# Decode attention for two models on one core: `wq` of B loaded ahead of the first block of keys, three products ahead of the first sum, and one tail transfer cut in two

## The chip, the cores and the metric

One core of a Trainium2 chip runs the whole program; the other cores are idle. The metric is the time of one execution on the device in microseconds (us). The core has five engines with queues of their own (TensorE or PE, VectorE or DVE, ScalarE or ACT, GpSimd or POOL, SyncE or SP) and a set of 16 DMA engines. They are ordered by semaphores alone: an instruction, or an engine's queue, waits until a counter has reached a value.

## The reference

Two independent attention layers, A and B, decode one token each: 32 heads of 128, a cache of 8192 keys and values per head, bf16.

```python
def attention(x, k_cache, v_cache, wq, wo):          # A and B alike
    q = (x @ wq).reshape(1, 1, 32, 128).transpose(0, 2, 1, 3)          # x: 1x1x512, wq: 512x4096
    scores = einsum("bhqd,bhkd->bhqk", q, k_cache) * 128 ** -0.5       # k_cache: 1x32x8192x128
    p = softmax(scores, axis=-1)
    o = einsum("bhqk,bhkd->bhqd", p, v_cache)
    return o.transpose(0, 2, 1, 3).reshape(1, 1, 4096) @ wo            # wo: 4096x512
out = concatenate([attention(A...), attention(B...)], axis=-1)         # 1x1x1024
```

With one query per head, every byte of the two caches is used once. The caches, `wq` and `wo` together are 285 MB.

## The kernel before, in words

The 64 heads are taken four at a time: 16 steps, called quads here (A's are 0 to 7, B's 8 to 15). A quad has 8.39 MB of keys (K0 to K15) and 8.39 MB of values (V0 to V15), each loaded with one DMA on SP's queue: 32 partitions per head, 256 cache positions per partition. `kn` holds two blocks of keys (even and odd quads), `vn` one block of values. Before the first values come, `vn` holds `wq` of A and of B (4.19 MB each), and a row at the start of the odd half of `kn` (`xrow`) holds `x` of A and B. At the end `wo` lies over `kn`.

What the engines do:

- **q.** In `pe_first`, PE spreads `x` over the partitions (line 326 before), ACT copies it to `xb` (354), and PE forms q of A and then of B with 16 matmuls for each half of the heads (336); after each half ACT copies the result to `qbc` (359, four copies), and PE's next half waits for these copies.
- **Scores of a quad.** DVE multiplies the keys with q in place in four chunks of 64 positions (`mul`, line 408). PE adds the products of one chunk with 16 matmuls against the identity (244 and 247) into one of two banks of `big`, and DVE adds up the last 8 columns into `s_sb` (`sr`, line 413). PE's chunk c waits for product c (`s_mul`) and for the `sr` that has freed its bank (`s_sr`).
- **Softmax.** DVE takes the maximum, ACT the exponentials (371).
- **Values.** After the score sums of quad n PE multiplies the probabilities of quad n-1 with its values (64 matmuls, line 294), ACT copies the result (365) and PE turns it into columns (300).
- **Output.** B's `wo` comes in six transfers (`WOB`); the last heads are multiplied in `rows` (219), after the last values.

SP's queue sets the order of the loads, and each load waits until its place is free: K(n+1) for the first product of quad n, V(n) for the value matmuls of quad n-1 (`s_pv`). At the start the order is `wq` of A, `x`, K0, `wq` of B (which waits for `wq` of A), K1 (which waits for the first product of quad 0), V0 (which waits for all of q, since `wq` lies in `vn`), K2 (which waits until all of quad 0 is summed, `s_red`, and K1 is there), V1, and so on. At the end V15 comes in two parts (`s_v` and `s_v1`, 192 and 64 positions), and PE waits for the second part after 48 of its 64 matmuls (`VCUT`).

The program text that the change touches, with the line numbers of the profile:

Of the kernel before, what the change touches and what calls it, by code (L numbers as in the profile page):

```python
# [11 lines left out]
P = 128  # L12


def bass_concat_heads__mha_block_cached__gqa_block_cached__decode_kernel(
# [18 lines left out]
    NA = 2  # L34
# [7 lines left out]
    G = 4  # L42
# [19 lines left out]
    RG = [32, 16, 8, 4, 2]  # L62
    VCUT = T - CT
# [3 lines left out]
    with ExitStack() as st:  # L67
# [53 lines left out]
        s_x, s_w, s_k, s_v, s_v1, s_out = [sem("s_" + x) for x in ("x", "w", "k", "v", "v1", "out")]  # L121
# [50 lines left out]
        def load_k(n, *needs):  # L172
            load(flat(kn[:, (n % 2) * T:(n % 2 + 1) * T, :]), quad(ks, n), s_k, *needs)
# [4 lines left out]
        def load_wq(a, *needs):  # L178
            load(flat(vn[:])[:, a * W:(a + 1) * W], wqs[a].rearrange("(p c) n -> p (c n)", p=P),
                 s_w, *needs)  # L180

        def load_wo(a, h0, n, c, *needs):
            load(wo_sb[:, a * H + h0:a * H + h0 + n, :].rearrange("p j n -> p (j n)"),
                 wos[a][h0 * Dh:(h0 + n) * Dh, :].rearrange("(p j) n -> p (j n)", p=P), c, *needs)

        load_wq(0)
        for a in range(NA):
            load(xrow[0:1, a, :], xs[a][0], s_x)
        load_k(0)
        load_wq(1, (s_w, 16))  # L190
        for n in range(NM):
            if n + 1 < NM:
                load_k(n + 1, *([(s_red, RED), (s_k, 32)] if n == 1 else [(s_mul, NCH * n + 1)]))
                load_v(n, (s_pv, n + 1) if n else (s_q, 4 * NA * 2))
# [5 lines left out]
        for (h0, n), c in list(zip(WOB, s_wo))[1:]:  # L200
            load_wo(1, h0, n, c)
# [6 lines left out]
        with nc.body("pe_main", valid_engines=[nc.tensor.engine]):  # L208
# [26 lines left out]
            with e.Fori(0, NM + 1) as n:  # L235
# [48 lines left out]
                with e.If_ne(nr, 0):  # L284
                    e.wait_ge(s_p, n1)
                    e.matmul(misc[:, 0:G], ones_f[:], rsum[:], start=True, stop=True).then_inc(s_sum, 1)  # L286
                    e.wait_ge(s_v, rv)
                    for j in range(T // NT):
                        if j * NT == VCUT:
                            with e.If_eq(nr, NM):  # L290
                                e.wait_ge(s_v1, 16)
                        q = QB * (j % NP)
                        ts = slice(j * NT, (j + 1) * NT)
                        i = e.matmul(acc[q:q + NT * G, :], pt[:, ts, :].rearrange("p t g -> p (t g)"),  # L294
                                     vn[:, ts, :].rearrange("p t d -> p (t d)"), start=(j < NP),
                                     stop=(j >= T // NT - NP), skip_group_check=True)
                    i.then_inc(s_pv, 1)
                    e.wait_ge(s_acc, n1)
                    for t in range(NT):
                        i = e.matmul(tps[:, 0:G], acc_sb[:, t * Dh:(t + 1) * Dh],  # L300
                                     tsel[:, t * G:(t + 1) * G], start=(t == 0), stop=(t == NT - 1))
                    i.then_inc(s_turn, 1)
                e.reg_add(n1, n1, 1)
                e.reg_add(rv, rv, 16)
            e.wait_ge(s_wo[1], 16)
# [3 lines left out]
            e.wait_ge(s_wo[2], 16)  # L309
            rows(2)  # L310
            e.wait_ge(t_dve, 11)
            for g in range(3, len(WOB)):
                e.wait_ge(s_wo[g], 16)
# [3 lines left out]
        with nc.body("pe_first", valid_engines=[nc.tensor.engine]):  # L317
            for r, v in ((rw, 16), (rq, G)):
                e.reg_mov(r, v)
            e.sem_inc(s_sum, 1)  # L320
            e.sem_inc(s_turn, 1)
            e.wait_ge(s_x, 16 * NA)
# [67 lines left out]
        e.sem_inc(s_sr, 2)  # L390
        e.memset(acc, 0.0).then_inc(s_pv, 1)
# [8 lines left out]
        e.wait_ge(s_qc, 2 * G)  # L400
        with e.Fori(0, NM):
# [112 lines left out]
```

## Time and profile before

| | us |
|---|---|
| three runs, median (lowest, highest) | 683.68 (683.41 to 686.24) |
| the profiled execution | 683.11 |
| its span in the trace | 681.9 |
| PE busy | 405.0 (59%) |
| DVE busy | 338.9 (50%) |
| ACT busy | 80.9 (12%) |
| DMA queue of the loads: 285.22 MB | 97.1% of 16 engines' span |

The profiled execution is 0.57 us below the median of the runs, and 1.2 us of it lies outside the span. Times in the rows count from the span's start. In a timeline's row stand the start, the duration, the engine, the line, the operation, what it writes and reads, and how many were merged; in brackets stands how long the engine was idle before and what ended that. "SPq" is SP's queue as it issues a DMA. In a row of stretches stand the stretch, its length, each engine's busy time with its count of instructions, then the granted clock of PE (1.00 is full speed), the share of the DMA engines and their GB/s.

### The profile page before, as it was taken

What the parts mean: (1) busy time and instruction counts of PE and PEld (TensorE: products, weight loads), DVE (VectorE), ACT (ScalarE), POOL (GpSimd) and SP (SyncE); (2) the same over time, 40 slices, a digit from 0 to 9 for tenths busy, and PEclk for the clock granted to TensorE, in tenths of its full rate; (3) what the DMA queues carried; (4) which work ended last, traced back from release to release, by engine and by line L of the source; (5) the groups of instructions that cost most, each with busy time, mean ns of one, the idle gap of its engine ahead of it and who ended that gap; (6) DMA issues with size and microseconds to landing.
All of it is one profiled execution on the core that took longest, in us unless ns stands there. A gap on an engine that the chain in (4) does not pass through costs nothing.

```text
span 681.9 us, 8031 instructions
## 1 busy us (share of the span) xinstructions
PE 405.0 (59%) x2407; PEld 169.9 (25%) x2407; DVE 338.9 (50%) x218; ACT 80.9 (12%) x182; POOL 2.4 (0%) x13
## 2 busy tenths in 40 slices
PE   1526757755838284674728285573818375583886
PEld 0112223222313132231313132231313122231333
DVE  1040784916556280836547281835647291655600
ACT  1211011020020202010020202011020202002020
POOL 1000000000000000000000000000000000000000
PEclk9866879886859697796959678796958788685887
DMA  9999793999999999999999999999999999999997
GB/s 382 429 467 427 327 423 115 434 442 431 431 431 431 431 431 431 431 431 431 431 431 431 431 438 450 438 442 434 442 431 431 431 431 431 431 431 431 423 442 304
DMA packets 6064, 285.24 MB, mean 418 GB/s; under 512 B 683, under 2 KB 942, under 8 KB 1198
## 3 DMA queue, kind: packets, MB, share of 16 engines
q1 hardware_dynamic: 6056, 285.22, 97.1%
q8 instruction: 1, 0.02, 0.0%
q14 instruction: 1, 0.01, 0.0%
q10 hardware_dynamic: 6, 0.00, 0.0%
HBM read 285.21 MB, written 0.00 MB: 418 GB/s over the span
## 4 chain that ended last, share of the span: by engine, by line
DMA 74%; DVE 13%; PE 9%; issue 2%; ACT 1%; DVEq 0%; ACTq 0%; SPq 0%
DMA kn<-in_B_k_cache_dram 40%; DMA kn<-in_A_k_cache_dram 25%; DVE kn L408 12%; PE big L247 5%; DMA vn<-in_B_wq_dram 4%; DMA vn<-in_B_v_cache_dram 3%; DMA vn<-in_A_wq_dram 2%; PE big L336 2%; PE acc L294 1%; PE big L244 1%; ACT qbc L359 1%; PE tps L300 0%; PE yrow L219 0%; DVE s_sb L413 0%; DVEq L403 0%
## 5 line engine op out<-in xcount | busy, mean ns | idle before, releaser
L408 DVE TENSOR_TENSOR kn<-kn,qbc x64 | 281.5, 4419 | 123.5 <-DMA kn<-in_A_k_cache_dram 65.6
L247 PE MATMUL big<-kn,ident 128*128 x960 | 272.4, 431 | 0.0
L244 PE MATMUL big<-kn,ident 128*128 x64 | 28.5, 445 | 216.7 <-DVE kn L408 212.2
L247 PEld LDWEIGHTS big<-kn,ident 128*128 128x128 bf16 x960 | 103.6, 108 | 153.6 <-issue 101.0
L413 DVE TENSOR_REDUCE s_sb<-big 128x64 f32<-128x512 f32 x64 | 44.1, 689 | 115.4 <-PE big L247 115.4
L365 ACT COPY acc_sb<-acc 128x512 f32<-128x512 f32 x16 | 9.4, 586 | 478.8 <-PE acc L294 478.8
L244 PEld LDWEIGHTS big<-kn,ident 128*128 128x128 bf16 x64 | 6.3, 99 | 234.0 <-issue 231.8
L294 PE MATMUL acc<-vn,pt 128*16 128x512 bf16 x1024 | 58.5, 380 | 2.7 <-DMA vn<-in_B_v_cache_dram 2.7
L371 ACT ACTIVATE pt<-s_sb,negb 32x256 bf16<-32x256 f32 x64 | 54.8, 857 | 1.3
L433 DVE TENSOR_TENSOR oD<-tps,rinv 128x4 f32 x16 | 2.6, 162 | 75.8 <-PE tps L300 75.6
L336 PE MATMUL big<-vn,acc_sb 128*128 x64 | 21.1, 497 | 22.8 <-DMA vn<-in_B_wq_dram 13.4
L294 PEld LDWEIGHTS acc<-vn,pt 128*16 128x16 bf16 x1024 | 24.0, 89 | 29.2 <-issue 2.9
L300 PE MATMUL tps<-tsel,acc_sb 128*128 128x4 f32 x128 | 17.7, 262 | 11.0 <-ACT acc_sb L365 10.4
L300 PEld LDWEIGHTS tps<-tsel,acc_sb 128*128 128x128 f32 x128 | 16.3, 199 | 19.3 <-ACT acc_sb L365 17.9
L336 PEld LDWEIGHTS big<-vn,acc_sb 128*128 x64 | 7.6, 119 | 36.2 <-issue 33.5
L371 ACT ACTIVATION_READ_ACCUMULATOR pt<-s_sb,negb 32x1 f32 x64 | 15.9, 248 | 0.0
L359 ACT CAST qbc<-big 32x512 f32 x16 | 9.2, 577 | 36.6 <-PE big L336 36.3
L269 PE MATMUL big<-kn,o 128*1 x48 | 12.4, 421 | 0.0
L286 PE MATMUL misc<-rsum,ones_f 128*128 128x4 f32 x32 | 6.0, 259 | 6.9 <-issue 6.2
L367 ACT ACTIVATE negb<-gm 128x1 f32<-128x1 f32 x16 | 3.2, 203 | 48.3 <-DVE gm L436 48.3
L326 PE MATMUL misc<-ones_bf,kn 1*128 1x128 bf16 x4 | 0.6, 302 | 13.1 <-DMA kn<-in_B_x_dram 13.1
L286 PEld LDWEIGHTS misc<-rsum,ones_f 128*128 128x128 f32 x32 | 4.8, 188 | 13.8 <-issue 13.8
(48 smaller groups left out, 38.5 us busy)
## 6 DMA issues: line engine op xcount, KB each, us to landing
vn<-in_B_v_cache_dram SPq DMA_DIRECT2D x1, 6144.0 KB, 18.4
vn<-in_A_wq_dram SPq DMA_DIRECT2D x1, 4096.0 KB, 13.2
vn<-in_B_wq_dram SPq DMA_DIRECT2D x1, 4096.0 KB, 29.1
kn<-in_A_wo_dram SPq DMA_DIRECT2D x1, 4096.0 KB, 24.3
kn<-in_B_wo_dram SPq DMA_DIRECT2D x1, 2048.0 KB, 28.9
vn<-in_B_v_cache_dram SPq DMA_DIRECT2D x1, 2048.0 KB, 23.0
kn<-in_B_wo_dram SPq DMA_DIRECT2D x1, 1024.0 KB, 25.0
kn<-in_B_wo_dram SPq DMA_DIRECT2D x1, 512.0 KB, 25.8
```

Source lines behind the costliest of these rows:

```text
L244: e.matmul(o, ident[:], chunk(0), start=True, stop=False, skip_group_check=True)
L247: i = e.matmul(o, ident[:], chunk((1 + u) * DW), start=False, stop=(u == RU - 1), skip_group_check=True)
L269: i = e.matmul(y, o2[:, bass.ds(h + u, 1)], wo_sb[:, h + u, :], start=False, stop=False, skip_group_check=True)
L286: e.matmul(misc[:, 0:G], ones_f[:], rsum[:], start=True, stop=True).then_inc(s_sum, 1)
L294: i = e.matmul(acc[q:q + NT * G, :], pt[:, ts, :].rearrange("p t g -> p (t g)"), vn[:, ts, :].rearrange("p t d -> p (t d)"), start=(j < NP ...
L300: i = e.matmul(tps[:, 0:G], acc_sb[:, t * Dh:(t + 1) * Dh], tsel[:, t * G:(t + 1) * G], start=(t == 0), stop=(t == NT - 1))
L336: i = e.matmul(big[:, bass.ds(hh, 1), :].rearrange("p o (i d) -> p (o i) d", d=Dh), xb[:, a, c, :], wq_v[:, a, c, j, :, hh, :], start=(c = ...
L359: e.copy(qbc[q, bass.ds(j * 4, 4), :].rearrange("p i d -> p (i d)"), big[q, hh, :]).then_inc(s_qc, 1)
L365: e.copy(acc_sb[:], acc).then_inc(s_acc, 1)
L371: i = e.activation(pt[q, :, h], s_sb[q, :], AF.Exp, bias=negb[q, :], scale=scale, accum_out=rsum[q, h:h + 1])
L408: e.tensor_tensor(k, k, qbc[:, bass.ds(n, 1), :].broadcast_to([P, CT, Dh]), ALU.mult).then_inc(s_mul, 1)
L413: e.tensor_reduce(s_sb[:, c * CT:(c + 1) * CT], big[:, c % 2, :].rearrange("p (t d) -> p t d", d=DW), AX.X, ALU.add).then_inc(s_sr, 1)
```

## The change

Six things change.

1. SP issues `wq` of B directly behind `x` and ahead of K0, without a wait. Each `wq` has a semaphore of its own, and so has K0 (`s_k0`). K1 waits only until PE has read `x` (`s_xm`), since `xrow` lies where K1 goes; it no longer waits for a product of quad 0.
2. PE waits for `wq` of A, and in the loop for `wq` of B, with the same loop over A and B as before; DVE waits for K0 before its loop over the quads.
3. In every quad DVE makes three products ahead of its first `sr`, and the fourth between the first and the second `sr`.
4. At the end PE issues eight matmuls of a zero column ahead of the wait for the second part of V15.
5. B's `wo` of heads 24 to 27 comes in two transfers: rows 0 to 119 of the partitions and rows 120 to 127.
6. PE waits for 32 instead of 16 on that part of `wo`.

On SP the first loads stand in this order; the names are the tile that is written and the tensor that is read, and in brackets the semaphores that the load waits for. Before:

```order
L170 DMA vn<-in_A_wq_dram 128x16384 [waits barrier_Pool_Activation_PE_DVE_SP_release]
L170 DMA kn<-in_A_x_dram 1x512
L170 DMA kn<-in_B_x_dram 1x512
L170 DMA kn<-in_A_k_cache_dram 128x32768
L170 DMA vn<-in_B_wq_dram 128x16384 [waits s_w]
L170 DMA kn<-in_A_k_cache_dram 128x32768 [waits s_mul]
L170 DMA vn<-in_A_v_cache_dram 128x32768 [waits s_q]
L170 DMA kn<-in_A_k_cache_dram 128x32768 [waits s_k,s_red]
L170 DMA vn<-in_A_v_cache_dram 128x32768 [waits s_pv]
```

And after:

```order
L173 DMA vn<-in_A_wq_dram 128x16384 [waits barrier_Pool_Activation_PE_DVE_SP_release]
L173 DMA kn<-in_A_x_dram 1x512
L173 DMA kn<-in_B_x_dram 1x512
L173 DMA vn<-in_B_wq_dram 128x16384
L173 DMA kn<-in_A_k_cache_dram 128x32768
L173 DMA kn<-in_A_k_cache_dram 128x32768 [waits s_xm]
L173 DMA vn<-in_A_v_cache_dram 128x32768 [waits s_q]
L173 DMA kn<-in_A_k_cache_dram 128x32768 [waits s_k,s_red]
L173 DMA vn<-in_A_v_cache_dram 128x32768 [waits s_pv]
```

`wq` of B has moved ahead of K0 and has lost its wait, K1 waits for `s_xm` in place of `s_mul`, and K2 and V1 wait for what they waited for.

On DVE the body of the loop over the quads is, before (`kn<-kn,qbc` is a product, `s_sb<-big` an `sr`):

```order
L408 TENSOR_TENSOR kn<-kn,qbc 128x8192
L408 ISA
L408 TENSOR_TENSOR kn<-kn,qbc 128x8192
L413 TENSOR_REDUCE s_sb<-big 128x64 [waits s_red,s_p]
L416 ISA
L408 TENSOR_TENSOR kn<-kn,qbc 128x8192
L413 TENSOR_REDUCE s_sb<-big 128x64 [waits s_red]
L416 ISA
L408 TENSOR_TENSOR kn<-kn,qbc 128x8192
L413 TENSOR_REDUCE s_sb<-big 128x64 [waits s_red]
```

And after:

```order
L427 TENSOR_TENSOR kn<-kn,qbc 128x8192
L427 ISA
L427 TENSOR_TENSOR kn<-kn,qbc 128x8192
L427 ISA
L427 TENSOR_TENSOR kn<-kn,qbc 128x8192
L432 TENSOR_REDUCE s_sb<-big 128x64 [waits s_red,s_p]
L435 ISA
L427 TENSOR_TENSOR kn<-kn,qbc 128x8192
L432 TENSOR_REDUCE s_sb<-big 128x64 [waits s_red]
L435 REGISTER_ALU
L432 TENSOR_REDUCE s_sb<-big 128x64 [waits s_red]
```

The third product has moved ahead of the first `sr`, and the fourth ahead of the second.

On PE, in the last pass of the loop (`acc<-vn,pt` are the value matmuls), this stands now around the wait for the second part of V15:

```order
L309 MATMUL acc<-vn,pt 16x512 [waits s_v]
L309 MATMUL acc<-vn,pt 16x512 x47
L302 COMPARE_AND_BRANCH
L304 MATMUL big<-kn,zero 1x512 x8
L302 UNCONDITIONAL_BRANCH [waits s_v1]
L309 MATMUL acc<-vn,pt 16x512 x16
L315 MATMUL tps<-tsel,acc_sb 128x4 [waits s_acc]
```

The row of eight matmuls is new; nothing else on PE has moved.

The diff, without the renaming of semaphores:

```diff
+    WP = {2: 120}
 ...
         def load_k(n, *needs):
-            load(flat(kn[:, (n % 2) * T:(n % 2 + 1) * T, :]), quad(ks, n), s_k, *needs)
+            load(flat(kn[:, (n % 2) * T:(n % 2 + 1) * T, :]), quad(ks, n), s_k if n else s_k0,
+                 *needs)
 ...
-        def load_wo(a, h0, n, c, *needs):
-            load(wo_sb[:, a * H + h0:a * H + h0 + n, :].rearrange("p j n -> p (j n)"),
-                 wos[a][h0 * Dh:(h0 + n) * Dh, :].rearrange("(p j) n -> p (j n)", p=P), c, *needs)
+        def load_wo(a, h0, n, c, *needs, p=slice(0, P)):
+            load(wo_sb[p, a * H + h0:a * H + h0 + n, :].rearrange("p j n -> p (j n)"),
+                 wos[a][h0 * Dh:(h0 + n) * Dh, :].rearrange("(p j) n -> p (j n)", p=P)[p], c, *needs)
 ...
+        load_wq(1)
         load_k(0)
-        load_wq(1, (s_w, 16))
-        for n in range(NM):
-            if n + 1 < NM:
-                load_k(n + 1, *([(s_red, RED), (s_k, 32)] if n == 1 else [(s_mul, NCH * n + 1)]))
-                load_v(n, (s_pv, n + 1) if n else (s_q, 4 * NA * 2))
+        load_k(1, (s_xm, 2))
+        load_v(0, (s_q, 4 * NA * 2))
+        load_k(2, (s_red, RED), (s_k, 32))
+        load_v(1, (s_pv, 2))
+        for n in range(2, NM - 1):
+            load_k(n + 1, (s_mul, NCH * n + 1))
+            load_v(n, (s_pv, n + 1))
 ...
-        for (h0, n), c in list(zip(WOB, s_wo))[1:]:
-            load_wo(1, h0, n, c)
+        for g in range(1, len(WOB)):
+            cut = WP.get(g, P)
+            for p in ([slice(0, cut)] + [slice(cut, P)] * (cut < P)):
+                load_wo(1, *WOB[g], s_wo[g], p=p)
+
+        def got_wo(e, g):
+            e.wait_ge(s_wo[g], 32 if g in WP else 16)
 ...
                             with e.If_eq(nr, NM):
+                                for _ in range(8):
+                                    e.matmul(big[0:1, 0, :], zero[:], wo_sb[:, 0, :], start=True,
+                                             stop=True)
                                 e.wait_ge(s_v1, 16)
 ...
             e.wait_ge(s_xb, NA)
+            e.wait_ge(s_w[0], 16)
             with e.Fori(0, NA) as a:
-                e.wait_ge(s_w, rw)
+                e.wait_ge(s_w[1], rw)
 ...
+        e.wait_ge(s_k0, 16)
         with e.Fori(0, NM):
             e.wait_ge(s_k, rk)
 ...
             mul(0)
             mul(1)
+            mul(2)
             e.wait_ge(s_p, n1)
             sr(0)
-            mul(2)
+            mul(3)
             sr(1)
-            mul(3)
             sr(2)
             sr(3)
```

More of the change, by code (lines that the diff above doesn't have):

```diff
@@ L119, in sem @@
             return ec(nc.semaphore(name))
-        s_x, s_w, s_k, s_v, s_v1, s_out = [sem("s_" + x) for x in ("x", "w", "k", "v", "v1", "out")]
+        s_x, s_k0, s_k, s_v, s_v1, s_out = [
+            sem("s_" + x) for x in ("x", "k0", "k", "v", "v1", "out")]
+        s_w = [sem("s_w%d" % a) for a in range(NA)]
         s_woA = sem("s_woA")
@@ L317, in bass_concat_heads__mha_block_cached__gqa_block_cached__decode_kernel @@
         with nc.body("pe_first", valid_engines=[nc.tensor.engine]):
-            for r, v in ((rw, 16), (rq, G)):
+            for r, v in ((rw, 1), (rq, G)):
                 e.reg_mov(r, v)
```

10 lines of the change are left out of this document (6 added, 4 removed).

## The prediction

> **What bounds the kernel now.** I read the page first: its span and the row of the DMA engines in 40 slices.
>
> ```profile
> span 681.9 us, 8031 instructions
> ...
> DMA  9999793999999999999999999999999999999997
> ```
>
> The DMA engines are busy from end to end but for the sixth and seventh slices and the last. So I looked at these in stretches of 2 us, and at the long middle in one.
>
> ```profile
> 80.00:82.00 2.00, 2.00 (x10) 0.86 (x9) 0.13 (x1) 0.00 (x0) 0.00 (x0) 1.00 0.00 0
> ...
> 104.00:106.00 2.00, 1.64 (x7) 0.57 (x6) 2.00 (x2) 0.00 (x0) 0.00 (x0) 1.00 0.00 0
> ...
> 112.00:114.00 2.00, 2.00 (x44) 0.92 (x40) 0.00 (x0) 0.00 (x0) 0.00 (x0) 1.00 0.00 0
> ...
> 115.00:640.00 525.00, 309.72 (x1842) 130.56 (x1843) 288.13 (x164) 59.07 (x140) 0.00 (x0) 0.79 1.00 432
> ```
>
> No byte moves at 80 to 82 and at 104 to 114; from 115 on the engines stand at 1.00 and 432 GB/s, so nothing but fewer idle microseconds of the DMA engines can help there. Which loads came late is told by SP's issues, and the stream's pace by the chain that ended last (start, duration).
>
> ```profile
> 83.20 0.33 SPq L170 DMA_DIRECT2D kn<-in_A_k_cache_dram  x1
> ...
> 114.94 0.33 SPq L170 DMA_DIRECT2D vn<-in_A_v_cache_dram  x1
> ...
> 146.44 0.33 SPq L170 DMA_DIRECT2D vn<-in_A_v_cache_dram  x1
> ```
>
> ```profile
> 14.06 29.06 DMA vn<-in_B_wq_dram
> ...
> 122.09 34.10 DMA kn<-in_A_k_cache_dram
> ...
> 586.60 33.99 DMA kn<-in_B_k_cache_dram
> ```
>
> K2 (83.20) and V1 (114.94) are issued when nothing is left in the queue. The last two rows are the landings of K3 (156.19) and K15 (620.59): twelve quads in 464.40, thus 38.70 for 16.78 MB (one block 19.35). V1 and K3 took 156.19 - 114.94 = 41.25, so an issue into an empty queue costs 41.25 - 38.70 = 2.55 beyond the bytes. The first 16.78 MB (both `wq` and K0) had landed at 14.06 + 29.06 = 43.12.
>
> **The stream without a pause.** K1 would then land at 43.12 + 19.35 = 62.47, V0 at 81.82, K2 at 101.17, V1 at 120.52, K3 at 139.87, which is 16.3 before 156.19. For that K2 has to be issued by 81.82 - 2.55 = 79.27 and V1 by 98.62.
>
> **Loads at the start.** The order of `wq` and K0 changes no bytes; I cost it at nothing. `wq` of A is first as before, K0 lands at 43.12, and K1's wait on `x` is met when PE has read it, ahead of the row at 15.93 below; behind it on SP stand V0 and K2, which want to be issued far later.
>
> ```profile
> 15.93 5.36 PE L336 MATMUL big<-vn,acc_sb 128*128 x16 [1.75 <-issue]
> ...
> 24.87 1.02 PE L336 MATMUL big<-vn,acc_sb 128*128 x4 [3.58 <-issue]
> ...
> 30.77 2.38 ACT L359 CAST qbc<-big 32x512 f32 x4 [6.96 <-PE big L336]
> ...
> 33.67 8.76 DVE L408 TENSOR_TENSOR kn<-kn,qbc  x2 [29.56 <-DMA kn<-in_A_k_cache_dram]
> ...
> 44.00 4.98 PE L336 MATMUL big<-vn,acc_sb 128*128 x16 [13.36 <-DMA vn<-in_B_wq_dram]
> ...
> 62.74 0.60 PE L244 MATMUL big<-kn,ident 128*128 x1 [4.57 <-issue]
> ```
>
> q of A is ready at 30.77 + 2.38 = 33.15, and PE then waited for `wq` of B until 44.00; K0's products lay ready meanwhile and their sums began at 62.74. In the new order `wq` of B lands one K0 earlier, near 23.8, so PE goes on at once: 1.2 after the copies (the idle 3.58 less ACT's 2.38), at 34.4. From there to the first sum it takes what it took, 62.74 - 44.00 = 18.74: **first sum at 53.1**, 9.6 earlier. K0's three products (4.4 each, half of 8.76) run from 43.4 to 56.6, so the first lies ready; PE is the later one. V0, which waits for q, can go at some 50, before its need at 62.47 - 2.55 = 59.9.
>
> **Three products ahead.** A quad as it was, quad 0's end and quad 1:
>
> ```profile
> 68.64 3.40 PE L247 MATMUL big<-kn,ident 128*128 x15
> 68.70 0.69 DVE L413 TENSOR_REDUCE s_sb<-big 128x64 f32<-128x512 f32 x1 [26.27 <-PE big L247]
> ...
> 83.21 0.69 DVE L413 TENSOR_REDUCE s_sb<-big 128x64 f32<-128x512 f32 x1 [3.08 <-PE big L247]
> ...
> 85.38 8.76 DVE L408 TENSOR_TENSOR kn<-kn,qbc  x2 [0.51 <-issue]
> ...
> 90.17 0.60 PE L244 MATMUL big<-kn,ident 128*128 x1 [7.00 <-DVE kn L408]
> ...
> 96.07 0.69 DVE L413 TENSOR_REDUCE s_sb<-big 128x64 f32<-128x512 f32 x1 [1.93 <-PE big L247]
> ...
> 106.39 0.39 PE L244 MATMUL big<-kn,ident 128*128 x1 [0.74 <-DVE kn L408]
> ...
> 110.61 0.69 DVE L413 TENSOR_REDUCE s_sb<-big 128x64 f32<-128x512 f32 x1 [3.99 <-PE big L247]
> ...
> 111.26 3.63 PE L294 MATMUL acc<-vn,pt 128*16 128x512 bf16 x64
> ```
>
> PE's first chunk takes 5.9 to 6.0 (62.74 to 68.70, 90.17 to 96.07), a following one without a wait 3.5, one that waited 4.2 (106.39 to 110.61). DVE stood idle 1.93 ahead of the first `sr`; the third product fills that, and the price is that this `sr` can come later than its sums.
>
> Quad 0 new: chunks end at 59.1, 62.6 (its `sr` came at 59.8), 66.2, and the fourth, whose product ends at 64.2 and whose bank is freed at 64.9, at 70.0. Then K2 is issued: 9 us ahead of 79.27, so the pause at 80 to 84 goes.
>
> Quad 1 new: its first product starts 2.2 after (83.21 to 85.38), at 72.2; PE starts 4.8 later, at 77.0, and ends chunks at 82.9 and 86.5. Three products end at 85.4, the first `sr` at 86.1; third chunk to 90.3; fourth product to 90.5, `sr` to 91.2, fourth chunk from 91.5 to 95.7. From 85.38 to 110.61 it was 25.2, now 23.5: 1.7 shorter. The values of quad 0 end 4.3 after (111.26 + 3.63 - 110.61): **V1 issued at 100.0**, late by 1.4 against 98.62. K3 lands at 100.0 + 41.25 = 141.25: **14.9 earlier**. All later loads move with it if none is issued late: V2 was issued at 146.44, 7.2 ahead of need (156.19 - 2.55), and the same distance stays, since everything here moves together. In the later quads the 1.7 is hidden behind the stream.
>
> **Before V15.** V15 must reach the queue before B's first part of `wo` has landed.
>
> ```profile
> kn<-in_B_wo_dram SPq DMA_DIRECT2D x1, 2048.0 KB, 28.9
> ...
> kn<-in_B_wo_dram SPq DMA_DIRECT2D x2, 128.0 KB, 25.8
> ```
>
> ```profile
> 625.69 0.43 SPq L170 DMA_DIRECT2D kn<-in_B_wo_dram  x1
> ...
> 650.63 0.80 SPq L170 DMA_DIRECT2D vn<-in_B_v_cache_dram  x2
> ...
> 651.47 2.34 SPq L170 DMA_DIRECT2D kn<-in_B_wo_dram  x5
> ```
>
> That part lands at 625.69 + 28.9 = 654.6; V15 is issued at 650.63, 1.4 ahead of need (654.6 - 2.55 = 652.0), and quad 15, shorter by 1.7 or more, only adds to this. No gain and no loss. The added issue on SP is one more of 0.43 behind 651.47, over 20 us before the data come.
>
> **The tail.**
>
> ```profile
> 115.58 1.06 PE L300 MATMUL tps<-tsel,acc_sb 128*128 128x4 f32 x8 [0.69 <-ACT acc_sb L365]
> ...
> 669.12 2.77 PE L294 MATMUL acc<-vn,pt 128*16 128x512 bf16 x48 [0.30 <-DMA vn<-in_B_v_cache_dram]
> 674.24 1.32 PE L294 MATMUL acc<-vn,pt 128*16 128x512 bf16 x16 [2.35 <-DMA vn<-in_B_v_cache_dram]
> ...
> 676.24 1.87 PE L300 MATMUL tps<-tsel,acc_sb 128*128 128x4 f32 x8 [0.68 <-ACT acc_sb L382]
> ...
> 680.22 0.29 DVE L477 CAST out_q<-yrow 128x128 bf16<-128x128 f32 x1 [0.82 <-PE yrow L219]
> ```
>
> ```profile
> 672.00:674.00 2.00, 0.00 (x0) 0.00 (x0) 0.00 (x0) 0.00 (x0) 0.00 (x0) 1.00 0.94 397
> 674.00:676.00 2.00, 1.32 (x16) 0.31 (x16) 0.00 (x0) 0.40 (x1) 0.00 (x0) 0.72 0.98 403
> ```
>
> PE idles 2.35 ahead of V15's last part, the granted clock falls to 0.72 in the next stretch, and the eight column matmuls take 1.87 against 1.06 in quad 0. The new eight matmuls cost some 0.22 each (3.40 for 15), 1.8 from 671.89 on, and end 0.5 before the wait does, so they delay nothing. With the clock held, 0.8 goes in that row and a little in the others, but the last `wo` lands at 651.47 + 2.34 - 0.43 + 25.8 = 679.2 on the old time, and `out_q`, at 680.22 now, cannot begin before some 679.4. I take **0.7**, with ends 0 (clock falls anyway) and 1.1 (`wo` lands a little earlier too). The cut transfer has the same bytes; I cost it at nothing, and its bad end is a rival below.
>
> [...]
>
> **The sum.** 14.9 + 0.7 = 15.6. The profiled execution is 683.11, so 667.5 by its own time; it lies 0.57 below the median of the runs, and from 683.68 the sum gives 668.1. I say 668.0.
>
> **Rivals.**
>
> - *V1 comes in time.* If PE is 1.4 faster over the seven chunks up to V1 (its first chunk was 5.3 to 6.0 in the rows, a waiting one 3.5 to 4.2), no pause is left: 16.3 + 0.7 = 17.0, 666.7. Speaks for it: the margin is small. Against: DVE's products, which set quad 1 from its third chunk on, have no slack.
> - *V1 comes later still.* Should PE lose its clock again within quads 0 and 1, a following chunk takes 5.9 in place of 3.5; two such push V1 to 104.8 and the time to 672.9. For it: PE idles 4.5 ahead of quad 0 (row at 62.74). Against: once begun, chunks follow without a gap.
> - *The change doesn't do what it says.* If `wq` of B came no earlier for PE, the first sum would stay at 62.74, V1 would be at 109.6 and the gain 5.3 + 0.7: 677.7. Against it: the stream delivered in the order of issue (`wq` of B took 29.06, behind K0).
> - *The cut transfer goes slower than the whole one*, the case that ends on the other side. If 120 rows are not spread over the engines but go through one, 491,520 bytes at 432 / 16 = 27 GB/s take 18.2 where the whole part took 524,288 / 432 = 1.2 us. The end then waits for `wo` 17 longer: 683.68 - 14.9 + 17 = 685.8. Two engines would take 9.1 and leave 676.7; only one engine makes it slower than before. No row shows a transfer of 120 rows. [...]
>
> **How the numbers follow.** Forecast 0.61, V1 in time 0.21, V1 later 0.12, no earlier q 0.03, one engine 0.03. The range 665.8 to 670.8: below, V1 in time with 1.1 in the tail (666.3) and half a microsecond; above, V1 2 later than forecast and nothing in the tail (668.1 + 2.0 + 0.7); it leaves out most of the last three. A change of 0.5%, 3.4 us, is about what a measurement of this kernel can tell from none: faster by more 0.95, within 0.02, slower by more 0.03.
>
> **What would show it.** Right: no stretch without bytes at 80 to 84 and at most 2 us of it near 100; first sum near 53, K2 issued near 70, V1 near 100, K15 landed near 605.7; DVE's first `sr` of a quad directly behind three products; a granted clock of 1.00 in the last 10 us. Wrong: SP's V1 well after 102, a wait of PE for `wq` of B, or PE at the end waiting for `wo` for more than 1 us.

## The result, and the profile after

The changed kernel takes 674.12 us (median of 6 runs, 672.38 to 674.61) where the kernel before takes 683.70 in the same comparison: a ratio of 0.9849, interval 0.9829 to 0.987. It is faster, as forecast, by 9.6 us; the forecast was 15.6 and 668.0. Of one kernel below (the cut at row 96) a run of 1385.97, twice the time of its others, is left out.

The page of the changed kernel, span and the row of the DMA engines, and stretches of 2 us at the two places where no byte moved before. The columns of a stretch are its length, the busy time of PE, its weight loads, DVE, ACT and POOL, the granted clock, the DMA share and GB/s:

```profile
span 673.1 us, 8068 instructions
...
DMA  9999987999999999999999999999999999999898
```

```profile
80.00:82.00 2.00, 0.00 (x0) 0.00 (x0) 2.00 (x2) 0.83 (x2) 0.00 (x0) 0.50 1.06 459
...
97.00:99.00 2.00, 2.00 (x10) 0.79 (x9) 0.00 (x0) 0.00 (x0) 0.00 (x0) 1.00 0.83 360
99.00:101.00 2.00, 1.87 (x8) 0.57 (x6) 0.10 (x1) 0.00 (x0) 0.00 (x0) 1.00 0.00 0
101.00:103.00 2.00, 1.75 (x30) 1.00 (x34) 1.10 (x3) 0.00 (x0) 0.00 (x0) 1.00 0.00 0
103.00:105.00 2.00, 2.00 (x44) 0.79 (x32) 0.00 (x0) 0.00 (x0) 0.00 (x0) 1.00 0.00 0
```

The pause at 80 is gone. The stream runs dry near 98.6, where the forecast has V1's need, and a pause of over 6 us is left where the forecast left 1.4. SP's issues of K2 and V1 (start, duration), and from the chain that ended last the landings of K3 and K15:

```profile
75.40 0.33 SPq L173 DMA_DIRECT2D kn<-in_A_k_cache_dram  x1
...
105.23 0.33 SPq L173 DMA_DIRECT2D vn<-in_A_v_cache_dram  x1
```

```profile
112.38 33.97 DMA kn<-in_A_k_cache_dram
...
576.96 33.97 DMA kn<-in_B_k_cache_dram
...
641.91 29.12 DMA kn<-in_B_wo_dram
671.07 0.33 PE yrow L231 x3
671.42 0.29 DVE out_q L496
```

V1 goes at 105.23 instead of 114.94: 9.7 earlier, not 14.9. K15 lands at 576.96 + 33.97 = 610.93, 9.7 earlier than the 620.59 before. The end adds nothing to that: from K15's landing to `out_q` it was 680.22 - 620.59 = 59.63, and is 671.42 - 610.93 = 60.49. So the time splits into three pieces, and a run is told by two numbers: **V1** (when V1 is issued) and **the tail** (from K15's landing to `out_q`). The piece between them, V1 to K15's landing, is 505.6 to 506.6 in every kernel below, and from the start of `out_q` to the end it is 2.9 to 3.0.

| kernel | V1 issued | K15 landed - V1 | tail | profiled execution | median of the runs |
|---|---|---|---|---|---|
| before | 114.94 | 505.65 | 59.63 | 683.11 | 683.70 |
| forecast | 100.0 | 505.65 | 58.9 | 667.5 | 668.0 |
| changed | 105.23 | 505.70 | 60.49 | 674.37 | 674.12 |

The miss, 6.9 by the profiled executions, is 5.2 in V1 and 1.6 in the tail. The experiments take these one after the other.

### The profile page after: what moved, and what is told of

Same layout as the page of the kernel before. It is cut to its first block, busy times and chain, and to the rows that moved or that the text cites. A ratio compares the mean times of both kernels' runs of the same rounds, so it can differ in the third digit from the quotient of the medians.

```text
span 673.1 us, 8068 instructions
## 1 busy us (share of the span) xinstructions
PE 405.5 (60%) x2415; PEld 168.2 (25%) x2415; DVE 337.0 (50%) x218; ACT 80.9 (12%) x182; POOL 2.4 (0%) x13
## 3 DMA queue, kind: packets, MB, share of 16 engines
q1 hardware_dynamic: 6063, 285.22, 98.5%
## 4 chain that ended last, share of the span: by engine, by line
DMA 72%; DVE 11%; PE 10%; issue 4%; ACT 1%; SPq 1%; DVEq 0%; ACTq 0%
DMA kn<-in_B_k_cache_dram 40%; DMA kn<-in_A_k_cache_dram 25%; DVE kn L427 10%; PE big L259 5%; DMA kn<-in_B_wo_dram 4%; PE big L353 4%; DMA kn<-in_B_x_dram 2%; ACT qbc L376 1%; PE acc L309 1%; DVE s_sb L432 1%; SPq L173 1%; PE big L256 0%; DVEq L422 0%; PE tps L315 0%; ACT acc_sb L371 0%
## 5 line engine op out<-in xcount | busy, mean ns | idle before, releaser
L259 PE MATMUL big<-kn,ident 128*128 x960 | 266.3, 419 | 0.0
L256 PE MATMUL big<-kn,ident 128*128 x64 | 28.1, 440 | 216.5 <-DVE kn L427 196.4
L259 PEld LDWEIGHTS big<-kn,ident 128*128 128x128 bf16 x960 | 100.8, 105 | 149.7 <-issue 99.4
L432 DVE TENSOR_REDUCE s_sb<-big 128x64 f32<-128x512 f32 x64 | 42.7, 686 | 73.4 <-PE big L259 73.4
L256 PEld LDWEIGHTS big<-kn,ident 128*128 128x128 bf16 x64 | 6.3, 98 | 234.8 <-issue 232.9
L309 PE MATMUL acc<-vn,pt 128*16 128x512 bf16 x1024 | 60.5, 387 | 2.4 <-DMA vn<-in_B_v_cache_dram 2.4
L353 PE MATMUL big<-vn,acc_sb 128*128 x64 | 25.2, 579 | 12.9 <-issue 12.9
L315 PE MATMUL tps<-tsel,acc_sb 128*128 128x4 f32 x128 | 16.9, 255 | 11.1 <-ACT acc_sb L382 10.4
L315 PEld LDWEIGHTS tps<-tsel,acc_sb 128*128 128x128 f32 x128 | 15.5, 191 | 19.1 <-ACT acc_sb L382 17.9
## 6 DMA issues: line engine op xcount, KB each, us to landing
kn<-in_B_wo_dram SPq DMA_DIRECT2D x1, 2048.0 KB, 28.9
```

Source lines behind the costliest of these rows:

```text
L256: e.matmul(o, ident[:], chunk(0), start=True, stop=False, skip_group_check=True)
L259: i = e.matmul(o, ident[:], chunk((1 + u) * DW), start=False, stop=(u == RU - 1), skip_group_check=True)
L315: i = e.matmul(tps[:, 0:G], acc_sb[:, t * Dh:(t + 1) * Dh], tsel[:, t * G:(t + 1) * G], start=(t == 0), stop=(t == NT - 1))
L353: i = e.matmul(big[:, bass.ds(hh, 1), :].rearrange("p o (i d) -> p (o i) d", d=Dh), xb[:, a, c, :], wq_v[:, a, c, j, :, hh, :], start=(c = ...
L432: e.tensor_reduce(s_sb[:, c * CT:(c + 1) * CT], big[:, c % 2, :].rearrange("p (t d) -> p t d", d=DW), AX.X, ALU.add).then_inc(s_sr, 1)
```

## The experiments

### The parts alone

Two kernels make one part of the change in the kernel before. The first has the order of `wq` of B and K0 with its waits; the second has three products ahead of the first `sr`:

```diff
+        load_wq(1)
         load_k(0)
-        load_wq(1, (s_w, 16))
...
+        load_k(1, (s_xm, 2))
```

```diff
             mul(1)
+            mul(2)
             e.wait_ge(s_p, n1)
             sr(0)
-            mul(2)
-            sr(1)
             mul(3)
+            sr(1)
```

> The kernel before with the order of wq and K0 alone changed (and the waits that belong to it): two products ahead, no columns, wo whole. Theory: V1 moves from 114.94 to some 107.7, the hour that the changed kernel with two products had, and the whole stream with it: 684.2 - 7.2 = 677.0. Rival: the order of the loads gives less by itself, since PE's sums of quad 0 then wait for DVE's products: V1 at 110 or later, 679.3 or more.

> The kernel before with three products ahead of the first sum and nothing else. Theory: quads 0 and 1 set K2 and V1 there too; quad 0 is shorter by some 3 (all three products lie ready before PE begins), quad 1 by 1.8, so V1 is issued near 110 and the time is 679.5. By the prediction's own price of 1.7 for each quad: 680.8. Rival: PE sets both quads while it forms q late, and the time stays at 684.

And the changed kernel with the products in the old order:

> The changed kernel with two products ahead of the first sum again. Theory: quads 0 and 1 set V1, and each is longer by 1.7 to 2.4, so V1 is issued 3.4 to 4 us later, near 109, and the time is 677.8. Rival: the wait of PE for its own chunks hides the third product, V1 stays near 105 and the time at 674.1.

| kernel | K2 issued | V1 issued | tail | median (lowest to highest, runs) | ratio to before (interval) |
|---|---|---|---|---|---|
| before, `wq` order alone | 75.81 | 107.65 | 59.62 | 677.33 (675.89 to 677.84, 4) | 0.9895 (0.9868 to 0.9921) |
| before, three products alone | 81.43 | 111.26 | 58.91 | 679.26 (678.60 to 680.35, 4) | 0.9926 (0.9899 to 0.9952) |
| changed, two products ahead | 75.81 | 107.66 | 60.40 | 678.03 (676.93 to 679.28, 4) | 0.9913 (0.9888 to 0.9938) |

From K2 to V1 it is 31.7 to 31.9 with two products ahead (31.74 before) and 29.8 with three: quad 1 is 1.9 shorter, and quad 0 gains as much alone (83.20 to 81.43). The order of the loads alone takes K2 from 83.20 to 75.81. The parts are worth 6.7 and 4.7 us in the medians (683.99 before in that comparison), and the medians of all three kernels came within 0.4 of what was expected (V1 within 1.4). The tail is already seen here to be 60.4 with the rest of the change and 58.9 to 59.6 without it.

### Why V1 came at 105: the clock in q

The theory behind this run: PE's clock is low through the q halves because PE idles some 3.5 us between them, and matmuls that fill these idles hold it. The filler writes a bank that is written again later, and reads tiles that are not used yet:

```diff
+            def busy(n):
+                for _ in range(n):
+                    e.matmul(yrow, ones_bf[:], pt[:, 0:P, :].rearrange("p t g -> p (t g)"),
+                             start=True, stop=True)
+
+            e.wait_ge(c_pool, POOL)
+            busy(36)
             e.wait_ge(s_x, 16 * NA)
...
+            busy(6)
...
+                    busy(8)      # behind each q half
```

> The changed kernel with PE kept busy through the forming of q: 36 matmuls of zeros ahead of x, 6 behind it, and 8 behind each of the four halves of q, into a bank that is overwritten later. Nothing else is changed. Theory: V1 is late by 5 us against the forecast because PE forms all four halves of q at half its clock (6.1 to 6.5 us each); at full clock a half takes 3.6, the first sum begins near 48, V1 is issued near 97, ahead of its need at 98.6, and no pause of the DMA engines is left: 667.5. Rival: a half takes 6 us for another reason (the weights, the copies), or the matmuls of zeros delay it; then V1 stays at 105 or later, and the time is 674 to 677.

PE's rows of the changed kernel, the four q halves, the first sum and the first of the fourth chunk (in brackets the idle time before, and what ended it), and stretches inside the second half of A and the second half of B:

```profile
15.95 6.08 PE L353 MATMUL big<-vn,acc_sb 128*128 x16 [1.74 <-issue]
25.60 6.37 PE L353 MATMUL big<-vn,acc_sb 128*128 x16 [3.57 <-issue]
36.06 6.26 PE L353 MATMUL big<-vn,acc_sb 128*128 x16 [4.09 <-issue]
45.86 6.48 PE L353 MATMUL big<-vn,acc_sb 128*128 x16 [3.54 <-issue]
56.91 0.60 PE L256 MATMUL big<-kn,ident 128*128 x1 [4.57 <-issue]
...
71.22 0.39 PE L256 MATMUL big<-kn,ident 128*128 x1 [0.62 <-issue]
```

```profile
26.00:28.00 2.00, 2.00 (x6) 0.67 (x5) 0.00 (x0) 0.00 (x0) 0.00 (x0) 0.50 1.21 524
...
46.00:48.00 2.00, 2.00 (x6) 0.72 (x6) 2.00 (x1) 0.00 (x0) 0.00 (x0) 0.50 1.06 459
```

The same with the idles filled (the first two rows are each the first quarter of a half, four matmuls; the second stretch lies inside the first chunk of sums):

```profile
25.07 1.02 PE L362 MATMUL big<-vn,acc_sb 128*128 x4 [1.85 <-issue]
...
34.16 1.02 PE L362 MATMUL big<-vn,acc_sb 128*128 x4 [2.37 <-issue]
...
52.20 0.39 PE L256 MATMUL big<-kn,ident 128*128 x1 [2.85 <-issue]
52.44 5.26 PE L259 MATMUL big<-kn,ident 128*128 x15
```

```profile
26.00:28.00 2.00, 1.40 (x7) 0.57 (x6) 0.00 (x0) 0.00 (x0) 0.00 (x0) 1.00 1.21 524
...
54.00:56.00 2.00, 2.00 (x6) 0.76 (x5) 2.00 (x1) 0.00 (x0) 0.00 (x0) 0.50 1.06 459
```

No half waits for its weights: between two halves PE waits for ACT's copies (2.38), and its own issue ends each idle, in both kernels (`issue`: the engine waited for nothing that the profile shows). With the idles at 1.8 to 2.4 the granted clock is 1.00 in this run where it was 0.50 (26 to 28 and 46 to 48), a half goes from 6.1 to 6.5 down to 5.0 (four times 1.02 and gaps of 0.3), and the first sum comes at 52.20, not 56.91. Behind the idle of 2.85 ahead of it the clock reads 0.50 at 54 to 56, and that chunk takes 5.5. V1 goes at 100.57, K2 at 70.71, and the median is **670.01 (669.97 to 670.45, 5 runs), ratio 0.9792 (0.9773 to 0.9811)**: 4.1 below the changed kernel. I had expected V1 at 97 and 667.5, with halves of 3.6; the gaps within a half stay at full clock, so that the direction was right and V1 gained 4.7 of the 8.2.

How long q takes also moves V1 from one execution to the next. Five kernels have the unfilled q and the same code up to V1: the four halves together take 23.0 (`wo` whole), 23.2 (cut at 112), 23.8 (no columns), 25.2 (the changed one) and 25.5 (cut at 127), and V1 is issued at 102.80, 103.15, 103.86, 105.23 and 105.56, thus 79.8 to 80.1 more than this sum in all five. Eight with filled q issue it between 100.26 and 101.10. The filling doesn't bring every half down in each of them: in this kernel and one more all four halves take 5.0, and in the six others one half (with the cut at 96, two) takes 5.3 to 5.8, behind an idle of 1.9 to 2.4. In the third half of one of these, the kernel without columns, the first four matmuls still take 1.02 and the next twelve 4.44 (3.6 in this kernel):

```profile
33.84 1.02 PE L359 MATMUL big<-vn,acc_sb 128*128 x4 [2.32 <-issue]
35.18 4.44 PE L359 MATMUL big<-vn,acc_sb 128*128 x12 [0.31 <-issue]
```

The granted clock at 36 to 38 is 0.50 there. The spread of the runs is not all from q: those of the changed kernel spread over 2.2 us and those of this one over 0.5, but those of the other filled kernels over 0.2 to 2.0, and V1 to K15's landing is 506.2 to 506.6 in three of them; why is not shown.

In the changed kernel the granted clock reads 0.50 from 24.5 to 31.1, 34.7 to 41.4, 45.0 to 51.6 and 55.2 to 61.8, which is most of three halves and of the first chunk, and 1.00 at 31.3 to 34.5, 41.5 to 44.8 and 51.8 to 55.0, where PE is busy for 0.5 to 0.8 us each time. The runs don't give one length of idle that brings it down: it reads 0.50 with idles of 3.5 to 4.1 and behind the one of 2.85, and with those of 1.9 to 2.4 all four halves took 5.0 in two kernels but not in the six others. Why one execution of the same code has a longer q than the next is not shown.

One more kernel, with `wo` whole (next part), had ten more matmuls behind the last half, ahead of PE's jump to the sums:

```diff
+            busy(10)
```

> The kernel with both edits (PE busy through q, wo whole), and ten more matmuls of zeros behind the last half of q, ahead of PE's jump to its main loop. Theory: the first chunk of quad 0 took 5.3 at a granted clock of 0.50 to 0.84 after an idle 2.85; held at full speed it takes 3.6, V1 moves from 100.6 to some 98.9, and the time is 1.7 less than with both edits alone: about 665.5. Rival: the fourth product on DVE or the jump sets quad 0, V1 stays at 100, and the time is the same within 0.5.

It gives 668.58 (667.89 to 669.90, 5 runs), ratio 0.9769 (0.9748 to 0.9789), where the kernel without these ten gives 668.91: no difference. I had expected 665.5; the rival, the same within 0.5, came. Its first chunk takes 3.6 now instead of 5.5, but K2 goes at 70.44 and V1 at 100.26, within 0.8 of the 71.15 and 101.01 without them. Its second and third chunks of quad 0 begin so:

```profile
56.73 0.39 PE L256 MATMUL big<-kn,ident 128*128 x1 [0.62 <-issue]
...
61.49 0.39 PE L256 MATMUL big<-kn,ident 128*128 x1 [0.62 <-issue]
```

The chunks begin 4.2, 4.8 and 4.8 apart, although the third product was there at 56.99 and the bank free at 57.59. So PE's own issue sets quad 0 here, and from the first sum to K2 it is 17.9 with a fast first chunk and 18.5 with a slow one.

### The tail: the cut of `wo`

The changed kernel with that part of `wo` whole:

```diff
-    WP = {2: 120}
+    WP = {}
```

> The changed kernel with one edit: wo of B's heads 24 to 27 comes whole again, 128 rows. Theory: the cut costs the end of the wo stream about 1.3 to 1.6 us, and the end waits for that stream, so the last wo lands near 669.5 in place of 671.03, out_q begins near 670, and the time is 672.8 (1.3 less than the changed kernel's 674.1). Rival: the wo stream is slower for another reason (the column matmuls, or the engines of the DMA at that hour), and the time stays at 674.1.

It takes 671.09 (670.19 to 673.26, 5 runs), ratio 0.9813 (0.9791 to 0.9836). V1 is at 102.80 in its profile, 2.4 earlier since its q halves took 2.2 less, so the median's 3.0 is not all the cut's. The tail tells the two apart: K15 lands at 608.44, `out_q` is at 667.31, 58.87 against 60.49. Its end, from the chain:

```profile
664.56 1.07 PE tps L315 x8
...
666.26 0.18 PE big L224
666.44 0.85 PE yrow L231 x27
667.31 0.29 DVE out_q L496
```

PE and DVE follow each other without a wait for `wo`; in the changed kernel the last row of PE waits for the last transfer of `wo` (the chain above).

Is it the cut at 120, or any cut? My guess, which no row shows, was that a transfer of 120 rows goes over 15 engines and one of 8 rows over 8, so that the shares of the engines become uneven; cuts at 112, 96 and 64 leave both parts a multiple of 16. And a cut at 127 asks for the case that the prediction feared.

```diff
-    WP = {2: 120}
+    WP = {2: 112}     # and, each in a kernel of its own, 127
```

> The changed kernel with the cut at 112 in place of 120: transfers of 112 and of 16 rows, as many transfers as before, both of a multiple of 16 rows. Theory 1, the cut costs because of the number of engines (15 and 8 in place of 16): with 16 for both, the wo stream is as fast as whole, the last wo 5.1 behind V15's last part, and the time is 671.1 to 671.5. Theory 2, one more transfer or an uneven share of rows costs: the last wo is 6 or more behind, and the time 673 to 674.

> The changed kernel with the cut at 127: transfers of 127 rows and of 1 row. This is the prediction's rival of one engine, made on purpose: if a transfer of 127 rows goes through one engine, 520 KB at 27 GB/s take 19.3 in place of 1.2, and the time is 674 + 17 = 691, the last wo some 23 behind V15's last part. If the number of rows does not set the number of engines, it stays at 674.

The next four share the filled q (with the ten matmuls behind it) and have no column matmuls; the first leaves `wo` whole, the others cut it.

> The kernel with PE busy through q and up to its jump, and wo whole, now without the eight columns. Theory: with V1 early PE's 48 matmuls run at a low clock and the columns only stand in the way of the last 16; without them these begin at the landing, and the end comes 1 earlier: 667.6. Rival: without them the clock is low in the eight column matmuls behind and the gain is given back: 668.6.

> The kernel without columns (PE busy through q, wo otherwise whole) with the cut at 120. The last wo then sets the end. Theory 1, 15 engines with another share of rows are slow: the last wo lands 29.2 to 29.5 after its issue in place of 27.9, and the time is 1.5 to 2 more than without the cut. Theory 2, one transfer more costs: the same here, so it is told apart by the next two.

> The same with the cut at 96: transfers of 96 and 32 rows, both of a multiple of 16. Theory 1 (the engine count of 15): 27.9 to 28.1. Theory 2 (one transfer more): 28.3 or more. [...]

> The same with the cut at 64: two transfers of 64 rows, both of a multiple of 16. Theory 1 (the engine count of 15): as without the cut, the last wo 27.9 to 28.1 after its issue. Theory 2 (one transfer more): 28.3 or more, as with the cut at 112. [...]

From the chains that ended last, the last transfer of `wo` that PE waits for; whole, then cut at 120 and at 64 (all filled), and the changed kernel cut at 127, where it is the transfer of 127 rows itself:

```profile
637.53 28.01 DMA kn<-in_B_wo_dram
```

```profile
637.71 29.01 DMA kn<-in_B_wo_dram
```

```profile
637.97 28.67 DMA kn<-in_B_wo_dram
```

```profile
640.85 46.00 DMA kn<-in_B_wo_dram
```

| `wo` of heads 24 to 27 | K15's landing to that of the `wo` in this row | tail | median (lowest to highest, runs) | ratio (interval) |
|---|---|---|---|---|
| filled q, whole | 58.71 | 59.05 | 668.41 (667.60 to 668.76, 5) | 0.9771 (0.9754 to 0.9787) |
| filled q, 120 and 8 | 59.98 | 60.38 | 670.22 (669.99 to 670.43, 4) | 0.9800 (0.9782 to 0.9819) |
| filled q, 96 and 32 | 59.90 | 60.30 | 669.27 (669.20 to 670.26, 3) | 0.9785 (0.9762 to 0.9808) |
| filled q, 64 and 64 | 60.27 | 60.67 | 669.68 (669.40 to 670.12, 4) | 0.9791 (0.9772 to 0.9810) |
| changed, 112 and 16 | 59.35 | 59.75 | 672.52 (671.61 to 674.61, 5) | 0.9838 (0.9816 to 0.9861) |
| changed, 120 and 8 | 60.10 | 60.49 | 674.12 (672.38 to 674.61, 6) | 0.9849 (0.9829 to 0.9870) |
| changed, 127 and 1 | 75.60 | 77.28 | 691.51 (one run) | |

Between the filled kernels only the cut differs. It makes the last `wo` land 1.2 to 1.6 later against the landing of K15, and the runs 0.9 to 1.8 longer. The cut at 112 costs less: its tail is 0.9 longer than that of the changed kernel with `wo` whole (58.87), and its median lies between the two theories' times. So a cut that keeps both parts at a multiple of 16 rows costs too: uneven shares are not what it needs. The cut at 127 costs 77.28 - 60.49 = 16.8 more than that at 120, where the forecast for one engine was 17, and while PE waits for it the DMA engines stand at a sixteenth:

```profile
678.00:686.00 8.00, 0.00 (x0) 0.00 (x0) 0.00 (x0) 0.00 (x0) 0.00 (x0) 0.50 0.06 26
```

The pages also count the packets of this queue: 6056 in every kernel with `wo` whole, 6063 in every one cut at 120 (7 more), 6072 at 112, 96 and 64 (16 more) and 6042 at 127 (14 fewer). The packets under 512 B alone make these differences: 683, 690, 699 and 669. My estimate from these counts is one small packet for each engine of a transfer: 15 + 8 in place of 16 at 120, 16 + 16 at 112, 96 and 64, and 1 + 1 at 127. At 127 the share of a sixteenth says the same. At 112, 96 and 64 each part would have 16 engines, and by the count of engines alone these cuts would have cost nothing; their tails are 0.9 to 1.6 longer.

Nor do the engines stand idle behind a cut. The same stretch of the filled kernels, whole and then cut at 120 (K15 landed at 606.83 and 606.74):

```profile
662.00:663.00 1.00, 0.80 (x8) 0.81 (x8) 0.00 (x0) 0.14 (x1) 0.00 (x0) 1.00 0.98 395
```

```profile
662.00:663.00 1.00, 0.89 (x8) 0.89 (x8) 0.00 (x0) 0.06 (x1) 0.00 (x0) 1.00 1.05 238
```

From 662 to 665 the share stays near 1.0 and the bytes come at 181 to 238 GB/s with the cut at 120, 223 to 315 at 96 and 188 to 256 at 64. From issue to landing the last transfer takes 28.0 whole, 29.0 (120), 28.7 (96) and 28.7 (64): the three cut ones are in line with one transfer more (28.3 or more). What slows the bytes behind a cut these runs do not show; it stays open.

### The tail: the column matmuls

The changed kernel without the eight column matmuls, and the kernel before with nothing but them:

```diff
-                                for _ in range(8):
-                                    e.matmul(big[0:1, 0, :], zero[:], wo_sb[:, 0, :], start=True,
-                                             stop=True)
                                 e.wait_ge(s_v1, 16)
```

> The changed kernel without the eight matmuls of the zero column. Theory: the end waits for the last part of wo, so the columns buy nothing now: 674.1 within 0.5, the last wo at the same distance of 6.7 us behind V15's last part. Rival: the columns delay the last 16 value matmuls by 0.45 and that is on the path: 673.6; or they hold the clock and that is on the path: 674.9.

> The kernel before with the eight matmuls of the zero column ahead of the wait for V15's last part and nothing else. Theory, as predicted: there the 48 matmuls run at full clock and end 2.4 before that part lands, so the columns fit, the clock holds, the eight column matmuls behind them take 1.06 in place of 1.87, and out_q begins 0.7 to 0.8 earlier behind V15's last part: 683.5. Rival: the clock falls all the same, or the columns delay the last 16: no change, or 0.4 more.

Before with the columns: 683.88 (682.04 to 686.27, 12 runs), ratio 0.9995 (0.998 to 1.001). Its timeline does what the forecast said:

```profile
672.35 1.89 PE L292 MATMUL big<-kn,zero 128*1 128x512 bf16 x8
674.87 1.04 PE L297 MATMUL acc<-vn,pt 128*16 128x512 bf16 x16 [0.63 <-DMA vn<-in_B_v_cache_dram]
676.60 1.05 PE L303 MATMUL tps<-tsel,acc_sb 128*128 128x4 f32 x8 [0.69 <-ACT acc_sb L385]
```

The matmuls of `tps` take 1.05, not 1.87, and the tail is 58.91, 0.72 shorter than 59.63; that is 0.1% of the time, and the 12 runs cannot tell it. In the changed kernel the same rows read:

```profile
659.47 4.33 PE L309 MATMUL acc<-vn,pt 128*16 128x512 bf16 x48 [2.43 <-DMA vn<-in_B_v_cache_dram]
663.63 1.46 PE L304 MATMUL big<-kn,zero 128*1 128x512 bf16 x6
664.71 0.39 PE L309 MATMUL acc<-vn,pt 128*16 128x512 bf16 x3
...
667.08 1.06 PE L315 MATMUL tps<-tsel,acc_sb 128*128 128x4 f32 x8 [0.70 <-ACT acc_sb L399]
```

PE now waits 2.43 for V15's first part (0.30 before), since it reaches that wait earlier against the stream; the 48 matmuls take 4.33 instead of 2.77, and the columns lie in the way: they start at 663.63, and without them the last 16 start 53.63 behind K15's landing, here 664.56. The three products alone bring this wait, as quad 15 is shorter (the changed kernel with two ahead waits 0.40, and its 48 take 2.77); the kernel before with nothing but the three has:

```profile
665.38 4.37 PE L294 MATMUL acc<-vn,pt 128*16 128x512 bf16 x48 [2.42 <-DMA vn<-in_B_v_cache_dram]
```

The changed kernel without the columns:

```profile
663.07 1.04 PE L306 MATMUL acc<-vn,pt 128*16 128x512 bf16 x16 [0.72 <-DMA vn<-in_B_v_cache_dram]
664.80 1.05 PE L312 MATMUL tps<-tsel,acc_sb 128*128 128x4 f32 x8 [0.69 <-ACT acc_sb L396]
...
668.52 1.35 PE L231 MATMUL yrow<-kn,oz 128*32 128x128 bf16 x32 [1.83 <-DMA kn<-in_B_wo_dram]
```

Behind the 48 matmuls, late and slow, `tps` takes 1.05 without the columns too; the last 16 start on the landing; and then PE waits 1.83 for the cut `wo`. The tail is 60.48 against 60.49, the median 672.99 (672.38 to 674.99, 4 runs), ratio 0.9841 (0.9814 to 0.9867). Its profiled execution is 1.5 shorter, of which V1 (103.86) makes 1.4. So here the columns buy nothing, and the cut hides what they cost (the last 16 end 0.8 later with them, counted from K15's landing).

With `wo` whole and q filled that cost could be seen. Filled q with `wo` whole and the columns, and the same with twelve columns moved ahead of V15's first part beside the eight (it has the ten matmuls behind q as well):

```diff
+                    for _ in range(12):
+                        e.matmul(big[0:1, 0, :], zero[:], wo_sb[:, 0, :], start=True, stop=True)
```

> The changed kernel with PE kept busy through the forming of q as in the run before, and wo of heads 24 to 27 whole: both edits together. Theory: the two losses are independent, one at V1 (4.1 in the medians) and one in the tail (3.0): 674.1 - 4.1 - 3.0 = 667.0, and within 1 of the forecast's 668.0. Rival: they overlap (the tail hides part of the other), and it stays at 669 to 670.

> The kernel with PE busy through q and up to its jump, and wo whole, and with twelve more matmuls of the zero column at the end, ahead of the wait for V15's first part. Theory: in the tail PE idles 1.3 to 2.8 ahead of V15's first part, the clock falls, the 48 value matmuls take 5.2 in place of 2.8, and the eight columns then run into the landing of V15's last part, which makes the last 16 late by 1.4. With the clock held the 48 take 2.8, the 16 begin within 0.4 of the landing, and the time is 0.9 to 1.4 less: 667.4. Rival: the end waits for the last wo anyway, and it stays within 0.4 of 668.6.

The first gives 668.91 (668.60 to 669.92, 5 runs), ratio 0.9770 (0.9751 to 0.9788), 1.9 more than expected; its 48 matmuls are slow:

```profile
655.76 5.30 PE L309 MATMUL acc<-vn,pt 128*16 128x512 bf16 x48 [1.34 <-DMA vn<-in_B_v_cache_dram]
```

The second gives 668.38 (668.27 to 668.45, 5 runs), ratio 0.9761 (0.9740 to 0.9783). There V15's 48 matmuls take 2.77 again:

```profile
655.13 2.77 PE L311 MATMUL acc<-vn,pt 128*16 128x512 bf16 x48
...
660.24 1.04 PE L311 MATMUL acc<-vn,pt 128*16 128x512 bf16 x16 [0.62 <-DMA vn<-in_B_v_cache_dram]
```

Its tail is 58.80 against 59.62 in the kernel that differs from it by these twelve alone (668.58 above), but it ends on the landing of the last `wo` (637.32 + 27.75 = 665.07, `out_q` at 665.40), and no columns at all give 59.05 and 668.41 (667.6 was expected, 668.6 was the rival). In the time these three (668.58, 668.38, 668.41) cannot be told apart; the twelve moved the end from PE to the last `wo`, as their rival had it, and gained nothing that shows.

## Why the prediction was right or wrong

**Right: which wait ends last.** The stream is the bound, its pauses at K2 and V1 are what can be won, and a microsecond of V1 is a microsecond of the end: V1 to K15's landing is 505.65 before, 505.70 after. K2 at 75.40 stays ahead of its need, 79.27, and the pause at 80 is gone.

**Wrong by 3.8: "From there to the first sum it takes what it took, 62.74 - 44.00 = 18.74."** It took 56.91 - 36.06 = 20.85, all of the 2.1 in the two halves of B (12.7 instead of 10.6; the idles of 3.54 and 4.57 are those of before). The start of it was 1.7 later than 34.4 as well: 36.06, mostly since q of A was ready only at 32.11 + 2.38 = 34.49, not 33.15. I had copied durations from a PE that stood still for 13.36 in the middle of q, and took them for those of four halves in a row. In the new rhythm of 6 us of work and 3.5 to 4.1 of idle the clock was 0.50 in most of the work of three halves (24.5 to 31.1, 34.7 to 41.4, 45.0 to 51.6). The idles were in the rows I quoted (3.58, 3.54); I used them for the start of PE and not for its clock. The clock was a rival, but with its place in quads 0 and 1 and a chance of 0.12 (672.9); it was in q, ahead of them. The filled kernel shows the size: with the clock at 1.00 in the stretches read (26 to 28, 44 to 52), the first sum comes at 52.20, 4.7 earlier, and V1 as much. That V1 is then at 100.57, so near the forecast's 100.0, is in part luck: the first sum is 0.9 ahead of its 53.1, and quad 0 takes 1.6 longer (next). For the first half (6.08 against 5.36) the granted clock reads 1.00 in both kernels; filling brought it to 5.0, but why it was slow the column does not show.

**Wrong by 1.6: quad 0.** From the first sum to K2 it took 18.5, forecast 16.9. The first chunk was as priced (56.91 to 62.83), but the third took 4.1 (66.46 to 70.60) and the fourth 4.2 (71.22 to 75.40) behind a gap of 0.62, against 3.6 and 3.8 in the forecast. I took "a following one without a wait 3.5" from chunks that followed a slow one; such a chunk only catches up. PE's own issue lets chunks begin some 4.8 apart, as the kernel with ten more matmuls shows, and here from the first on (56.91, 66.46 two later, 71.22 three later). Neither the fourth product nor its bank held the fourth chunk back (there at 68.13 and 68.72).

**Right: quad 1.** 29.83 from K2 to V1, forecast 30.0. All of V1's 5.2 lies ahead of K2.

**Right: V15 ahead of need.** SP's issues of the first part of B's `wo` and of V15:

```profile
616.03 0.43 SPq L173 DMA_DIRECT2D kn<-in_B_wo_dram  x1
...
638.90 0.80 SPq L173 DMA_DIRECT2D vn<-in_B_v_cache_dram  x2
```

With the 28.9 that this part of `wo` takes as before, V15 was needed at 616.03 + 28.9 - 2.55 = 642.4; it went 3.5 earlier. But "No gain and no loss" missed what a shorter quad 15 does behind this: PE waits 2.4 for V15's first part instead of 0.3, its clock falls (0.50 at 660 to 662), and the 48 matmuls take 4.3 instead of 2.8.

**Wrong by 1.6: the tail.** "The cut transfer has the same bytes; I cost it at nothing": it costs 1.3 with all else equal (tails 59.05 and 60.38) and 1.6 in the changed kernel (58.87 and 60.49). I had put the danger in one engine, which is real at 127 rows (a share of 0.06, a tail of 77.28), and had no case for a loss between nothing and that of two engines (8 to 9). "End 0.5 before the wait does, so they delay nothing" was right for the kernel before and wrong here: they ran past the landing. The 0.7 that I gave the columns is real where they stand alone (0.72), and in the changed kernel it comes with `wo` whole (59.63 to 58.87), but without columns too (59.05 there, 58.91 with the three products alone).

The sum: V1 5.2 and the tail 1.6 are 6.8 of 6.9. With both set right, q filled and `wo` whole, the kernel takes 668.4 (0.9771, 0.9754 to 0.9787, without columns), 5.7 below the changed one and at the forecast's time. No kernel tried is measurably better than that.

## What to carry to other kernels

When a change closes a long wait, the work around it gets a new rhythm of bursts and idles: take durations for it from rows with that rhythm, or price them at the clock that such a rhythm had here (0.50), and put the idles between the bursts into the sum. Work that fills an idle ahead of a wait has to be placed anew when the stream ahead of it shifts, and a small load cut in two, in the queue that ends the program, had a cost of its own here with the same bytes (0.9 to 1.6 in the tail). Splitting the time at two or three events (here V1's issue and K15's landing) shows which kernels differ where, even if their totals are blurred by something else.

## What the runs showed that was not expected

- With idles of 3.5 to 4.1 us between bursts of 6, PE's granted clock reads 0.50 in the stretches above. With the idles filled down to 1.8 to 2.4 us it reads 1.00 in the stretches above, and all four halves take 5.0 in two kernels; in six others one or two of the four take 5.3 to 5.8 (0.50 at 36 to 38 in one). It reads 0.50 behind an idle of 2.85 too (54 to 56), and behind one of 2.43 ahead of V15 (660 to 662, with the 48 matmuls in 4.33 instead of 2.77).
- The same code up to V1 issues it anywhere from 102.8 to 105.6, by how long the four halves of q take (23.0 to 25.5); with q filled, within 0.8 us.
- In quad 0 PE's chunks begin 4.2 to 4.8 apart by its own issue where they wait for nothing; a first chunk of 3.6 instead of 5.5 brought K2 only 0.6 nearer to the first sum.
- A 512 KB load cut in two, both parts a multiple of 16 rows, makes the last `wo` land 1.2 (96 and 32) to 1.6 us (64 and 64) later, with the DMA engines busy meanwhile; a cut of 127 and 1 makes the tail 17 longer than one of 120 and 8, with a sixteenth of them busy.
